# Three filler matmuls tied ahead of Q, and a new order of the work, in a gated mix of memory attention and a ReGLU layer

## The chip, the cores and the metric

The kernel runs on one NeuronCore of one Trainium2 chip. The metric is the device time of one execution in microseconds, as a median over runs. The engines are TensorE (PE, with its weight loads as PEld), VectorE (DVE), ScalarE (ACT), GpSimd (POOL) and SyncE (SP, which here only issues DMAs). Each takes its own instructions in order and waits on semaphores for the others.

## The reference

One sequence of 2048 tokens with 512 features goes through two branches, and a gate per token mixes them.

```python
g = sigmoid((x * gate_w).sum(-1))              # one number per token
# branch A: 32 heads of 16, in 4 segments of 512 tokens, M and z carried along
a_dot = softmax(q k^T * scale + mask) v        # causal, within the segment
a_mem = (phi(q) M) / (phi(q) z + 1e-6)         # recall of the segments before
o = sigmoid(beta) * a_mem + (1 - sigmoid(beta)) * a_dot
M += phi(k)^T v;  z += phi(k).sum(tokens)      # after each segment
a = o @ wo                                     # phi(t) = t + 1 if t > 0 else exp(t)
# branch B
b = (relu(x W_gate) * (x W_up)) @ W_down       # 512 -> 1792 -> 512
out = g * a + (1 - g) * b
```

All inputs and the output are bf16; sums are made in fp32 in PSUM.

## The kernel before

The four segments are processed one after another. For a segment the kernel has these pieces, each a task for one engine:

- Q and K projections for four groups of eight heads (`proj_q`, `proj_k`): four matmuls of 128x512 each (L460, in `full`), copied out of PSUM by DVE (L556 to QT, L572 to ktr, L575 to the masked KT). phi of them is an exponential on ACT and two operations on DVE (L529, L530). phi of K is transposed by a DMA on SP's queue (L588, pkT to pK).
- V projections for four blocks of 128 tokens (`proj_v`, copied by L602).
- Scores: 16 small matmuls per group (L623, and L636 for half blocks on the diagonal), 32 rows of the array each and four side by side. ACT does the exponential of 128x2048 (L645, to E). PSUM banks 0 to 3 are theirs, so one group of scores follows the exponential of the one before.
- Products with V (L696, 17 columns of the array each, four side by side), normalised on DVE (L727, L735, L737, L732, L708).
- Memory: the update (L816, L832), the denominators (L752), which go to DRAM and come back spread over partitions (L770 stores `coefs`, L784 reloads it to `cdr` and `xn`), the recall (L792) and its multiply on DVE (L803).
- The gate per token from `xn`, the rows of x (L414), which is loaded again for each segment (L276).
- The ReGLU layer: 14 pieces of gate and up matmuls, ReLU on ACT (L860, to `rgr`), the product on DVE (L866, to `hT`, 14 buffers), and for each 128 tokens 14 matmuls on `wd_sb` and 4 on `wo_sb` into one bank, scaled by L892 and stored by SP (L897).

A full-width matmul that stands behind column-tiled work is emitted by `full` as four matmuls of 32 columns (L464) side by side instead of one of 128 (L460), so that the tiling of the array does not change there.

What runs when is set by a list written into the kernel. The tasks are numbered as they are added to `Plan`; `ORDER` is the list of these numbers, and `UNITS` has one character for every use of a buffer and says which one of its ring or which PSUM bank is taken. A planner, which is not in the file, has made both from the tasks' estimated durations and from `lat`, the time until a result is seen elsewhere. `Plan.run` follows the list and asserts that a task stands behind those that it depends on. The order across engines comes from semaphores alone.

At the start, x of the first segment and `wq` are loaded by SP and ACT in eight transfers; then SP issues wk, wv and the other weights. PE does seven matmuls on constants (`heat`, L911). `x0_tasks` (L489 on) then transposes x on PE: 16 matmuls with an identity in five tasks (`flip`, L497), each with a copy out of PSUM on DVE or ACT (L505). With the last one it adds a task `idle` with fillers, matmuls on a zeroed tile `junk` (L515) whose result nobody reads. Q of the first segment waits for these copies and for `wq`.

Of the kernel before, what the change touches and what calls it, by code (L numbers as in the profile page):

```python
# [12 lines left out]
P = 128  # L13
# [14 lines left out]
RH = 14  # L28

ORDER = """  # L30
# [62 lines left out]
"""  # L93

UNITS = (
    "765432100132020000013101220024300002310000001000000012000000000300010000320000101003220101"
    "1333037221411293125003a1206013d023c0128200b00110010001000003000101111202000012221300456102"
    "1000000300000002300000000200000000021000212021042231103832220016112b200332370109023d102522"
    "6c010a100010003030007050103121103020013433212012450011000003200000002300000000210002000001"
    "00022313012212031271013301542062134310a1029420b0218202c113d1100001030206070303030202331200"  # L100
    "004563201000003200000003200000000010000000760000134203022222121201602230025023a504c3137312"
    "83119407b625d00110112100"
)


class Slot:


    def __init__(self, cands):
        self.cands, self.units, self.left = tuple(cands), (), 0  # L110

    @property
# [66 lines left out]
def kernel(  # L179
# [15 lines left out]
    nc = tc.nc  # L195
# [7 lines left out]
    plan = Plan()  # L203
# [285 lines left out]
    def x0_tasks():  # L489
        got = []  # L490
        parts = [(0, 0, 4), (1, 0, 4), (2, 0, 4), (3, 0, 2), (3, 2, 4)]
        for n, (t, c0, c1) in enumerate(parts):
# [17 lines left out]
            if n == 4:  # L510
                js = work()

                def idle(js=js):
                    for h in range(2):
                        nc.tensor.matmul(bank(js)[:, 2 * P * h:2 * P * h + 2 * P],  # L515
                                         lhsT=junk[:, 0:P],
                                         rhs=junk[:, None, 0:P].to_broadcast([P, 2, P]), start=True,
                                         stop=True)
                plan.add("PE", 426, K(-9) + n + 0.5, idle, [a], lat=0, need=[js], frees=[js], size=4)
            got.append(b)  # L520
        x0_first.extend(got[0:2])
        return [got[0:4], got[0:3] + got[4:5]]

    def proj_mm(w, c, seg):
# [452 lines left out]
```

## Time and profile before

| | |
|---|---|
| median of three runs | 267.53 us (267.46 to 268.33) |
| the profiled execution's own time | 268.72 us |
| its span, first to last instruction | 266.8 us |
| PE busy | 258.2 us (97%) |
| DVE busy | 204.2 us (77%) |
| ACT busy | 182.3 us (68%) |
| POOL busy | 63.7 us (24%) |
| moved by DMA | 19.43 MB, mean 73 GB/s |

A view by stage gives the busy time of each engine in a stretch, with the count of its instructions. A timeline gives start and length of a run of like instructions; the bracket behind it is the idle time before, and what ended it. In a list of groups, a row has the line of the kernel, the engine, the operation, the tiles and shapes, the count, then the busy time, the mean duration of one in ns, and the idle time in front of them. Matmuls are pipelined, so that the duration of one is longer than the step from one to the next. Some 30 of the matmuls have no record in this trace.

### The profile page before, as it was taken

How to read it: one execution, taken by the hardware profiler on the slowest of the kernel's cores; microseconds unless marked ns; L12 is line 12 of the kernel's file. 1: busy time of each engine (PE TensorE's matmuls, PEld its weight loads, DVE VectorE, ACT ScalarE, POOL GpSimd, SP SyncE). 2: the span in 40 equal slices, each digit the busy share in tenths (PEclk: the TensorE clock that was granted, in tenths of full speed). 3: DMA queues.
4: the chain of work that ended last, by engine and by line, in shares of the span. 5: the costliest groups of instructions: out<-in, count | busy, mean ns of one | idle time of the engine just before them, and what ended most of it. 6: DMA issues, size and time to landing. Idle time of an engine off the chain costs nothing.

```text
span 266.8 us, 8499 instructions
## 1 busy us (share of the span) xinstructions
PE 258.2 (97%) x3647; PEld 120.2 (45%) x3677; DVE 204.2 (77%) x473; ACT 182.3 (68%) x168; POOL 63.7 (24%) x168
## 2 busy tenths in 40 slices
PE   7999999999999999999999999999999999999995
PEld 4534444454445444444444444454444444445454
DVE  3499999999969476759999895768978875759422
ACT  3089998998886789883867777767466867761200
POOL 8023734132213222231122221222012222220000
PEclk9999999999999999999999999999999999999999
DMA  6999980111413410001101213200200120300011
GB/s 189 328 260 336 237 192 2 23 25 33 92 30 74 144 45 22 2 2 37 46 19 29 47 42 105 78 22 2 78 2 5 58 86 22 104 6 5 2 39 39
DMA packets 30028, 19.43 MB, mean 73 GB/s; under 512 B 15016, under 2 KB 28456, under 8 KB 29992
## 3 DMA queue, kind: packets, MB, share of 16 engines
q1 hardware_dynamic: 29416, 18.38, 24.8%
q8 instruction: 28, 0.46, 0.7%
q10 hardware_dynamic: 576, 0.52, 0.7%
q14 instruction: 8, 0.07, 0.1%
HBM read 13.21 MB, written 2.55 MB: 59 GB/s over the span
## 4 chain that ended last, share of the span: by engine, by line
PE 86%; DVE 8%; issue 3%; DMA 2%; SPq 0%; ACT 0%; DVEq 0%; ACTq 0%
PE ps L460 53%; PE ps L464 16%; PE ps L623 7%; PE ps L696 7%; DVE junk L414 2%; DMA wq_sb<-in_A_wq_dram 2%; DVE ktr L572 1%; DVE hT L866 1%; DVE KT L575 1%; PE ps L636 1%; PE ps L816 1%; DVE gcat L391 1%; DVE Vp L602 0%; PE ps L792 0%; PE ps L752 0%
## 5 line engine op out<-in xcount | busy, mean ns | idle before, releaser
L645 ACT ACTIVATE E<-ps 128x2048 bf16<-128x2048 f32 x64 | 120.3, 1880 | 28.0 <-PE ps L623 24.8
L674 POOL TENSOR_SCALAR_AFFINE_SELECT E<-E 128x256 bf16<-128x256 bf16 x128 | 53.9, 445 | 171.0 <-ACT E L645 171.0
L460 PE MATMUL ps<-xT,wg_sb 128*128 128x512 bf16 x179 | 50.3, 380 | 0.6 <-issue 0.3
L866 DVE TENSOR_TENSOR hT<-ps,rgr 128x512 bf16<-128x512 f32 x56 | 37.7, 683 | 15.8 <-PE ps L460 9.5
L460 PE MATMUL ps<-xT,wu_sb 128*128 128x512 bf16 x165 | 45.9, 380 | 0.4 <-issue 0.2
L860 ACT ACTIVATE rgr<-ps 128x512 bf16<-128x512 f32 x56 | 32.8, 599 | 17.6 <-PE ps L464 9.8
L460 PE MATMUL ps<-wd_sb,hT 128*128 128x512 bf16 (+2 forms) x168 | 37.5, 344 | 0.5 <-issue 0.5
L727 DVE STREAM_TRANSPOSE T<-ps 128x512 f32<-128x512 f32 x32 | 22.0, 707 | 7.3 <-PE ps L696 7.0
L460 PEld LDWEIGHTS <-wg_sb 128*128 128x128 bf16 x186 | 17.1, 98 | 21.7 <-issue 3.0
L623 PE MATMUL ps<-QT,KT 32*128 32x320 bf16 (+3 forms) x512 | 25.4, 273 | 0.3
L460 PEld LDWEIGHTS <-wu_sb 128*128 128x128 bf16 x170 | 15.4, 98 | 19.4 <-issue 2.8
L892 DVE TENSOR_SCALAR osr<-ps,ngcol 128x512 bf16<-128x512 f32 (+2 forms) x18 | 12.4, 688 | 14.0 <-PE ps L460 10.5
L460 PEld LDWEIGHTS <-hT 128*128 128x128 bf16 x174 | 15.4, 98 | 16.0 <-issue 1.5
L464 PE MATMUL ps<-wd_sb,hT 128*32 128x512 bf16 x312 | 20.5, 379 | 0.0
L696 PE MATMUL ps<-E,Vp 128*17 128x320 bf16 (+3 forms) x512 | 19.2, 273 | 0.4 <-DVE ktr L572 0.3
L623 PEld LDWEIGHTS <-KT 32*128 32x128 bf16 x512 | 7.7, 92 | 25.9 <-issue 25.0
L460 PE MATMUL ps<-xT,wq_sb 128*128 128x512 bf16 (+1 forms) x64 | 17.0, 394 | 0.9 <-DMA wq_sb<-in_A_wq_dram 0.7
L645 ACT ACTIVATE Em<-ps 128x2048 bf16<-128x2048 f32 x8 | 15.0, 1881 | 4.1 <-PE ps L636 4.0
L460 PE MATMUL ps<-xT,wk_sb 128*128 128x512 bf16 x58 | 16.9, 379 | 0.3 <-issue 0.2
L460 PE MATMUL ps<-wv_sb,xT 128*128 128x512 bf16 x54 | 15.8, 380 | 0.6 <-issue 0.6
L572 DVE CAST ktr<-ps 128x512 bf16<-128x512 f32 x16 | 11.0, 686 | 4.4 <-PE ps L460 4.4
L464 PE MATMUL ps<-xT,wu_sb 128*32 128x512 bf16 x216 | 14.3, 379 | 0.0
(102 smaller groups left out, 298.2 us busy)
## 6 DMA issues: line engine op xcount, KB each, us to landing
out_dram<-osr SPq DMA_DIRECT2D x15, 128.0 KB
wd_sb<-in_B_W_down_dram SPq DMA_DIRECT2D x2, 896.0 KB
xn<-in_A_x_dram SPq DMA_DIRECT2D x3, 512.0 KB
xn<-coefs SPq DMA_DIRECT2D x6, 256.0 KB
cdr<-coefs SPq DMA_DIRECT2D x6, 256.0 KB
wg_sb<-in_B_W_gate_dram SPq DMA_DIRECT2D x2, 512.0 KB
wu_sb<-in_B_W_up_dram SPq DMA_DIRECT2D x2, 512.0 KB
wg_sb<-in_B_W_gate_dram SPq DMA_DIRECT2D x2, 384.0 KB
```

What stands on the lines that cost most here:

```text
L414: zs.append(plan.add("DVE", 690, key, lambda t=t: nc.vector.scalar_tensor_tensor(junk[:], xn[:, t, :], 1.0, gwb[:], ALU.mult, ALU.mult, ac ...
L460: nc.tensor.matmul(out, lhsT=lhsT, rhs=rhs, start=start, stop=stop)
L464: nc.tensor.matmul(out[r], lhsT=lhsT[:, r], rhs=rhs, start=start, stop=stop, tile_position=(0, 32 * j))
L572: d = plan.add("DVE", 600, key - RQK, lambda: nc.vector.tensor_copy(ktr[ks.i][:], bank(sl)), [a], DVL + 40, need=[ks], frees=[sl])
L623: nc.tensor.matmul(ps[:, j * L + o:j * L + o + L - q], lhsT=KT[i][rows, kb, 3 * r:3 * r + 2].rearrange("p h q -> p (h q)"), rhs=QT[i][rows ...
L645: last_exp[0] = [plan.add("ACT", 66 + 4 * L / 1.2, key, lambda: nc.scalar.activation(dst, ps[:, 0:4 * L], ACT.Exp, scale=SCALE), [a] + war ...
L674: nc.gpsimd.affine_select(out=m[:, :, o:o + HP], in_=m[:, :, o:o + HP], compare_op=ALU.is_ge, fill=0.0, base=HP, pattern=[[0, 4], [1, HP]] ...
L696: nc.tensor.matmul(bank(sl)[32 * m:32 * m + HW, q:q + w], lhsT=(Vp[i] if n < 4 else Vm)[:, kb, r, 4 * c + j, 0:HW], rhs=rhs, start=(n == 0 ...
L727: done.append(plan.add("DVE", 633, key - RL, lambda r=r, sl=sl: nc.vector.transpose(T[ts.i][:, r], bank(sl)), [a] + done, 75 if r else 0, ...
L860: r = plan.add("ACT", 478, key - RL, lambda sl=gsl, rs=rs: nc.scalar.activation(rgr[rs.i][:], bank(sl), ACT.Relu), [g], ACL, frees=[gsl])
L866: nc.vector.tensor_tensor(hT[hs1.i][:], bank(sl), rgr[rs.i][:], ALU.mult)),
L892: nc.vector.tensor_scalar(osr[os.i][:, n0 - c0:n1 - c0], bank(sl)[:, 0:n1 - n0], ngcol[:, tt:tt + 1], None, ALU.mult)),
```

## The change

The fillers: there are three matmuls of 256 columns instead of two, all into the same half of a bank; the planner's duration for them is 640 ns instead of 426. The task's handle `j` is added to `x0_first`, the list of tasks for which the first matmuls of Q wait in the plan, so that the fillers have to stand ahead of Q.

The order: `ORDER` and `UNITS` are made anew. The planner took later times for the results of other engines, and of the free buffers of a ring it took the one that had been free for longest. The matmuls, copies and transfers that are done stay the same apart from the fillers, but PE's instructions change in number, since other matmuls now stand behind column-tiled work (3677 matmuls become 3969).

```diff
 ORDER = """
-    0 1 2 3 4 5 6 7 8 9 10 11 12 13 14 15 16 17 18 19 20 21 22 26 670 23 27 29 28 33 31 30 34
-    35 32 63 36 76 89 50 90 51 52 91 53 77 78 92 54 79 55 67 56 37 68 59 60 58 102 57 69 116 64
...
+    0 1 2 3 4 5 6 7 8 9 10 11 12 13 14 15 16 17 18 19 20 21 22 26 670 23 27 29 28 33 35 30 31
+    34 37 36 32 76 89 50 51 77 52 78 53 90 91 79 54 55 92 63 80 56 105 81 59 60 57 108 58 82
...
 UNITS = (
-    "765432100132020000013101220024300002310000001000000012000000000300010000320000101003220101"
...
+    "456701230142303000031221111122121222030000003000000010011000002300020000230113110223100023"
...
                 def idle(js=js):
-                    for h in range(2):
-                        nc.tensor.matmul(bank(js)[:, 2 * P * h:2 * P * h + 2 * P],
-                                         lhsT=junk[:, 0:P],
+                    for h in range(3):
+                        nc.tensor.matmul(bank(js)[:, 0:2 * P], lhsT=junk[:, 0:P],
                                          rhs=junk[:, None, 0:P].to_broadcast([P, 2, P]), start=True,
                                          stop=True)
-                plan.add("PE", 426, K(-9) + n + 0.5, idle, [a], lat=0, need=[js], frees=[js], size=4)
+                j = plan.add("PE", 640, K(-9) + n + 0.5, idle, [a], lat=0, need=[js], frees=[js],
+                             size=6)
             got.append(b)
-        x0_first.extend(got[0:2])
+        x0_first.extend(got[0:2] + [(j, 0.0)])
         return [got[0:4], got[0:3] + got[4:5]]
```

More of the change, by code (lines that the diff above doesn't have):

```diff
@@ L30 @@
 ORDER = """
[62 rows of a table removed]
[62 rows of a table added]
 """
 UNITS = (
-    "765432100132020000013101220024300002310000001000000012000000000300010000320000101003220101"
[L97 to L102, printed above, removed]
+    "456701230142303000031221111122121222030000003000000010011000002300020000230113110223100023"
+    "135121300042016323701290018020d320a211b001c00111002222003003111322000222203122100214567302"
+    "1000003300000003201100000200003000001011303031023221103821070016002332053209102a3224113b02"
+    "1d213c011211002010120122032121202030212232003145670132000002200000003301100000010000000033"
+    "01101302038322101272209312232232036211a0115110b3024103d022c1002120132212242202021113315302"
+    "135671032000002300000002301100000320000000120110238012130303027200901220233212600053214300"
+    "a302d024b211c01101200110"
 )
```

120 rows, old and new, of the table ORDER are left out of this document.

## The prediction

> **What bounds the kernel now.** I read the page first, for the engines' shares.
>
> ```profile
> span 266.8 us, 8499 instructions
> PE 258.2 (97%) x3647; PEld 120.2 (45%) x3677; DVE 204.2 (77%) x473; ACT 182.3 (68%) x168; POOL 63.7 (24%) x168
> ```
>
> TensorE (PE) is busy for 97% of the span. A change can gain only where PE idles, where it runs slowly, or in the tail. The busy time by stage says where that is:
>
> ```profile
> core 0: us, PE busy (x) PEld busy (x) DVE busy (x) ACT busy (x) POOL busy (x), PEclk, DMA share, GB/s
> 0.00:10.00 10.00, 8.45 (x38) 4.85 (x39) 2.37 (x11) 2.24 (x3) 5.46 (x24) 1.00 0.76 225
> 10.00:20.00 10.00, 9.67 (x65) 4.28 (x66) 9.24 (x23) 6.45 (x8) 1.82 (x4) 1.00 1.12 294
> 30.00:60.00 30.00, 29.57 (x512) 13.61 (x509) 28.82 (x74) 28.16 (x30) 11.37 (x33) 1.00 0.34 69
> 120.00:150.00 30.00, 29.29 (x297) 12.78 (x299) 28.22 (x70) 21.06 (x23) 6.63 (x12) 1.00 0.15 40
> ```
>
> The first 10 us lack 1.55 us of PE. After that PE lacks 0.33 us in ten, then 0.4 to 0.7 in each 30. From 30 to 60 us DVE (28.8 of 30) and ACT (28.2 of 30) are nearly full too, and DVE is again from 120 to 150. So the head is worth a look, and then PE's order in time there:
>
> ```profile
> 0.84 2.93 PE L911 MATMUL ps<-const-bfloat16-1.0 128*128 128x512 bf16 x7 [0.84 <-PEq L961]
> 3.57 1.91 PE L497 MATMUL ps<-ident,xn 128*128 128x128 bf16 x16
> 6.19 4.92 PE L460 MATMUL ps<-xT,wq_sb 128*128 128x256 bf16 x20 [0.71 <-DMA wq_sb<-in_A_wq_dram]
> 10.96 1.46 PE L460 MATMUL ps<-xT,wk_sb 128*128 128x512 bf16 x6
> 12.25 0.38 PE L515 MATMUL ps<-junk 128*128 128x256 bf16 x2
> 12.69 0.38 PE L460 MATMUL ps<-xT,wk_sb 128*128 128x512 bf16 x1
> 12.90 0.59 PE L460 MATMUL ps<-wv_sb,xT 128*128 128x512 bf16 x2
> 13.62 0.40 PE L623 MATMUL ps<-QT,KT 32*128 32x448 bf16 x8
> ```
>
> PE warms itself, transposes x, idles 0.71 us until wq has landed, and does Q. The two fillers (junk) stand at 12.25 us, not in that gap. Now the same shape early and late, first between 6 and 10 us, then between 10.4 and 13 us (the last figure before the second bar is the mean duration of one):
>
> ```profile
> L460 PE MATMUL ps<-xT,wq_sb 128*128 128x256 bf16 x12 | 2.7, 419 | 0.7 <-DMA wq_sb<-in_A_wq_dram 0.7
> L460 PE MATMUL ps<-xT,wq_sb 128*128 128x512 bf16 x3 | 1.5, 634 | 0.0
> L460 PE MATMUL ps<-xT,wk_sb 128*128 128x512 bf16 x7 | 1.8, 379 | 0.1
> L460 PE MATMUL ps<-xT,wq_sb 128*128 128x256 bf16 x2 | 0.4, 273 | 0.0
> ```
>
> Until about 10 us PE runs at about half rate, although the table's PEclk says 1.00. Six matmuls on wk take 1.46 us and one alone 0.38, so each further one costs (1.46 - 0.38) / 5 = 0.216 us. From 6.19 to 10.96 us PE does 14 matmuls of 256 columns and 6 of 512, 13 times 512 columns: 13 x 0.216 = 2.81 us at the full rate. It took 4.77. **The half rate costs Q 1.96 us.** Twice that, 3.9 us, is how long it lasts: until 6.19 + 3.92 = 10.1 us.
>
> **The change, part by part.**
>
> *The fillers move.* Two, of 2 x 0.109 = 0.22 us, leave the path at 12.25 us. Three stand between the last transpose and Q. At half rate each costs about 0.216 us, 0.65 in all; the transposes end at 5.48 us and Q starts at 6.19, so 0.07 us of the gap is left and wq still sets Q's start. If wq came up to 0.6 us sooner, the cover would be gone and Q would be held for that long. The fillers also wait for DVE: their bank is that of the first x tile, which DVE copies out from 4.24 us on, three copies in 1.76 us, so it is free by 4.9, before they are due:
>
> ```profile
> 4.24 1.76 DVE L505 CAST xT<-ps 128x512 bf16<-128x512 f32 x3 [2.64 <-PE ps L497]
> 9.90 1.95 DVE L556 CAST QT<-ps 128x512 bf16<-128x512 f32 x3 [3.90 <-PE ps L460]
> 12.02 0.69 DVE L572 CAST ktr<-ps 128x512 bf16<-128x512 f32 x1 [0.17 <-PE ps L460]
> ```
>
> *The full rate comes earlier.* 4.6 us of PE work without a break (0.84 to 5.48) did not bring it; 3.9 us after the break (6.19 to 10.1) did. [...] Q then runs at half rate for 0 to 0.8 us, which costs 0 to 0.4 instead of 1.96: a gain of 1.55 to 1.95, I take 1.7, a little under the middle. [...]
>
> *What is late next.* wv. The order has V's first matmul after 14 of 256 and 12 of 512 columns of Q and K, 19 x 0.216 = 4.1 us: it is wanted at 10.3 to 10.7, where before it was at 12.90. Its landing is not shown. x, wq, wk and wv are 2.1 MB, and by the GB/s of these rows (123 for 3 us, 262 for 3 us, then us by us) they are in by 9.6, or by 11 if other traffic shares the queues:
>
> ```profile
> 0.00:3.00 3.00, 2.16 (x6) 0.81 (x7) 0.51 (x7) 0.32 (x1) 2.16 (x10) 1.00 0.38 123
> 3.00:6.00 3.00, 2.48 (x19) 1.79 (x17) 1.76 (x3) 1.92 (x3) 2.80 (x12) 1.00 0.96 262
> ...
> 9.00:10.00 1.00, 1.00 (x3) 0.30 (x2) 0.10 (x1) 0.00 (x0) 0.00 (x0) 1.00 1.02 352
> 10.00:11.00 1.00, 1.00 (x7) 0.59 (x6) 1.00 (x2) 0.00 (x0) 0.00 (x0) 1.00 1.08 383
> ```
>
> The wait is 0 to 0.7; I take 0.3. Queued behind it on PE are the rest of K and V and the first scores (L623). These wait for K's chain on DVE: K's last matmul, the 0.69 us copy, three KT scalings; from K's copy at 12.02 to scores at 13.62 it was 1.6 us. Now K ends after 12 of 256 and 10 of 512 columns, about 10.1 with 0.2 lost to the half rate, its copy starts at about 10.3, and the scores could start at 11.9, which PE reaches at 12.0 without and 12.3 with the wait. The 0.19 us by which PE waited there before (12.90 + 2 x 0.216 + 0.1 for the switch of tiling, against 13.62) goes. Head: -0.22 - 1.7 + 0.3 - 0.19 = **-1.8 us**.
>
> *The new order.* In the built programs PE's matmuls are the same in columns, and both change the tiling 152 times. Between the first nine score groups the old order has 77 matmuls of 512 columns in the eight gaps, 10 in most; the new one has 95, mostly 12 or 14. After the last score group 122 become 106. So work is spread forward.
>
> ```profile
> L645 ACT ACTIVATE E<-ps 128x2048 bf16<-128x2048 f32 x64 | 120.3, 1880 | 28.0 <-PE ps L623 24.8
> L860 ACT ACTIVATE rgr<-ps 128x512 bf16<-128x512 f32 x56 | 32.8, 599 | 17.6 <-PE ps L464 9.8
> 140.88 0.73 PE ps L696 x32
> ```
>
> A gap of 10 is 2.2 us of PE plus scores of about 0.4; ACT needs 1.88 for the exponential and mostly a 0.60 for something else, 2.5 in all. There was no slack, and now there is 0.4 to 0.8 per gap. The work moved forward also raises DVE's and ACT's load early, so it is not free. On SP's queue one key transpose (pK) now goes ahead of the reload of xn:
>
> ```profile
> 33.15 0.49 SPq L276 DMA_DIRECT2D xn<-in_A_x_dram  x1
> 39.39 0.67 DVE L414 SCALAR_TENSOR_TENSOR junk<-xn,gwb 128x512 bf16<-128x512 bf16 x1
> ```
>
> Until about 31 us weights fill the DMA queues, so SP does not run ahead with PE. xn comes some 1.2 us later, and its user on DVE, L414, is due about as much earlier: DVE may stop for up to 1 us there, in a stage where it is full. That is in the bounds below. From 10 to 264 us PE lacks 264 - 10 - (258.2 - 8.45) = 4.2 us of busy time, some of it records that are missing; 140.88, where DVE's chain hands back to PE, is the largest stop. All 4.2 is the most that can be won. A loss is not excluded; I bound it by one such DVE stage again, 2 us. I take **-0.4**, nearer to zero, because few of these stops exceed 0.3 us.
>
> 97 more full-width matmuls are done as four of 32 columns. I take 0 by these rows:
>
> ```profile
> 241.72 15.32 PE ps L464 x284
> L464 PEld LDWEIGHTS <-hT 128*32 128x32 bf16 x312 | 7.8, 97 | 6.5 <-issue 0.3 <-DVE hT L866 0.2
> 263.97 0.35 DVE osr L892
> ```
>
> 284 / 4 = 71 quartets in 15.32 us are 0.216 each, the same as one whole matmul. The end is alike: two 128-column copies and one small output transfer behind the last matmul, 266.8 - 264.0 = 2.8 us.
>
> **Sum.** -1.8 - 0.4 = -2.2 us. The profiled execution's own time is 268.72 us (span 266.8 and 1.9 around it), 1.2 over the median of the three runs, 267.53. It would become 266.5, and the median 265.3.
>
> **Rivals.**
>
> *The break still counts.* [...] Then only the fillers' 0.22 and the order's 0.4 are gained: 266.9. [...] Against: 0.07 left of 0.71. Chance 0.16.
>
> *Slower: the last coefficients.* The new order does the third segment's memory update some 44 us of PE work later, so that the fourth's denominators, their round trip by DRAM and the recall stand close. On SP's queue the last reload (L784) now also stands behind an output transfer.
>
> ```profile
> 226.49 0.57 SPq L770 DMA_DIRECT2D coefs<-dnr  x1
> 228.97 1.20 SPq L784 DMA_DIRECT2D xn<-coefs  x2
> 163.59 1.20 SPq L784 DMA_DIRECT2D cdr<-coefs  x2
> 168.00:169.00 1.00, 1.00 (x40) 0.48 (x29) 1.00 (x3) 0.79 (x1) 0.14 (x1) 1.00 0.59 203
> 238.85 0.37 PE ps L792 x16
> ```
>
> Before, 12.4 us lay between store and recall; now 9.4 of PE work do. From the last reload to its user on DVE (L803) there are 7.4, and a reload takes at most 4.4 or so to issue and land (those issued at 163.59 keep the queues busy to about 169, with what lay ahead of them). If it slips past L803, DVE, in order, holds the last hT products and PE's last matmuls. Spare are about 2 to 3 us; to end over 0.8 us slower the slip must pass some 3 + 2.2 + 0.8 = 6 us, giving 268.5 or more. Chance 0.08.
>
> *Slower: quartets cost.* [...] In this trace four loads of 32 columns take 4 x 7.8 / 312 = 0.10 us of the load path. Were they uncovered, 97 x 0.10 = 9.7 us would be lost; the gain is used up from 0.023 each. 0.216 against 0.216 speaks against it. Chance 0.04.
>
> **How the numbers follow.** The forecast has 0.70, 0.02 stays unnamed. Its own range is head -1.2 to -2.4 and order +0.8 to -1.2, ends that hardly fall together: 264.2 to 267.0. With the first rival's spread I give 264.1 to 267.4. About 0.3%, 0.8 us, can be told from no change. Faster: 0.70 x 0.95 + 0.16 x 0.4 = 0.73. Same: 0.13, mostly the first rival. Slower: 0.14, the rest.
>
> **What would show it.** Right: fillers right behind the transposes, a gap below 0.1 us before Q, 256-column matmuls of Q near 273 ns from about 7 us on, first scores near 12.3 us, and PE's lack after 10 us below 4.2. Wrong: matmuls of 634 ns still at 9 us (first rival); a wait of over 0.7 us for wv; DVE's L803 waiting for a DMA near 235 us; quartets over 0.216 us.

## The result, and the profile after

The changed kernel takes **265.0 us** (median of six runs, 264.45 to 265.43), the kernel before 267.69 us (six runs, 267.28 to 268.69). The ratio is 0.9894, with a 95% interval of 0.9872 to 0.9917. The profiled execution took 264.89 us, with a span of 263.2. The forecast was 265.3. The sum came out, and the experiments show that two of its terms did not: most of the gain is not where the forecast put it.

The page of the changed kernel, with the lines on the shares and the chain that ended last:

```profile
span 263.2 us, 9091 instructions
PE 255.8 (97%) x3941; PEld 118.8 (45%) x3969; DVE 204.4 (78%) x473; ACT 183.2 (70%) x168; POOL 61.9 (24%) x168
PE 90%; DVE 4%; DMA 3%; issue 1%; SPq 0%; DVEq 0%
```

PE is the bound as before. The timeline of PE in the head, and the groups of matmuls between 6 and 10 us (last figure before the second bar: mean ns of one):

```profile
3.57 1.71 PE L497 MATMUL ps<-ident,xn 128*128 128x128 bf16 x16
5.12 0.49 PE L515 MATMUL ps<-junk 128*128 128x256 bf16 x3
5.69 2.87 PE L460 MATMUL ps<-xT,wq_sb 128*128 128x256 bf16 x18
9.49 0.38 PE L460 MATMUL ps<-xT,wk_sb 128*128 128x512 bf16 x1
10.42 0.60 PE L460 MATMUL ps<-wv_sb,xT 128*128 128x512 bf16 x2 [0.55 <-DMA wv_sb<-in_A_wv_dram]
11.82 0.40 PE L623 MATMUL ps<-QT,KT 32*128 32x448 bf16 x8
```

```profile
L460 PE MATMUL ps<-xT,wq_sb 128*128 128x256 bf16 x13 | 1.9, 273 | 0.0
L460 PE MATMUL ps<-xT,wq_sb 128*128 128x512 bf16 x6 | 1.6, 379 | 0.0
```

At first sight it is what was forecast: the fillers stand behind the transposes, Q runs at 273 ns where it had run at 419, V waits for wv, and the first scores come at 11.8 us instead of 13.6. (The second matmul on wk has no record ahead of that wait, while other profiles of this order show two there; the wait is therefore nearer to 0.33 us than to the 0.55 of the row.) But the fillers took 0.49 us together, 0.109 from one to the next: they ran at the full rate already. From the last transposes on, the step from one to the next is 56 ns instead of 107; the full rate came at 4.9 us, ahead of the fillers. So this profile does not show that they brought it.

Behind the head, the busy time by stage:

```profile
core 0: us, PE busy (x) PEld busy (x) DVE busy (x) ACT busy (x) POOL busy (x), PEclk, DMA share, GB/s
0.00:10.00 10.00, 8.94 (x51) 4.97 (x52) 4.67 (x14) 2.14 (x3) 5.46 (x24) 1.00 0.76 235
30.00:60.00 30.00, 29.58 (x534) 13.70 (x540) 28.20 (x69) 26.51 (x26) 9.46 (x28) 1.00 0.38 73
120.00:150.00 30.00, 29.58 (x369) 12.84 (x362) 26.15 (x63) 20.98 (x22) 5.47 (x14) 1.00 0.22 56
```

DVE has more room where it was nearly full: 28.20 us instead of 28.82 from 30 to 60, 26.15 instead of 28.22 from 120 to 150, and ACT 26.51 instead of 28.16. The matmuls done as quartets cost nothing here either. This is a run of 44, and the group behind it:

```profile
247.01 2.55 PE L464 MATMUL ps<-wd_sb,hT 128*32 128x512 bf16 x44
249.38 1.03 PE L464 MATMUL ps<-wo_sb,oT 128*32 128x512 bf16 x16
```

Eleven quartets take 249.38 - 247.01 = 2.37 us, 0.215 each.

### The profile page after: what moved, and what is told of

Same layout as the page of the kernel before. It is cut to its first block, busy times and chain, and to the rows that moved or that the text cites. A ratio compares the mean times of both kernels' runs of the same rounds, so it can differ in the third digit from the quotient of the medians.

```text
span 263.2 us, 9091 instructions
## 1 busy us (share of the span) xinstructions
PE 255.8 (97%) x3941; PEld 118.8 (45%) x3969; DVE 204.4 (78%) x473; ACT 183.2 (70%) x168; POOL 61.9 (24%) x168
## 4 chain that ended last, share of the span: by engine, by line
PE 90%; DVE 4%; DMA 3%; issue 1%; SPq 0%; DVEq 0%
PE ps L460 48%; PE ps L464 24%; PE ps L623 8%; PE ps L696 7%; DMA wv_sb<-in_A_wv_dram 2%; DMA xn<-in_A_x_dram 1%; PE ps L636 1%; PE ps L816 1%; DVE KT L575 1%; DVE ktr L572 1%; DVE junk L414 1%; PE ps L752 1%; DVE hT L866 0%; DVE gcat L391 0%; PE ps L792 0%
## 5 line engine op out<-in xcount | busy, mean ns | idle before, releaser
L645 ACT ACTIVATE E<-ps 128x2048 bf16<-128x2048 f32 x64 | 120.1, 1876 | 31.3 <-PE ps L623 27.1
L674 POOL TENSOR_SCALAR_AFFINE_SELECT E<-E 128x256 bf16<-128x256 bf16 x128 | 52.6, 435 | 171.5 <-ACT E L645 171.4
L460 PE MATMUL ps<-xT,wg_sb 128*128 128x512 bf16 x144 | 40.6, 380 | 1.0 <-issue 0.5
L460 PE MATMUL ps<-wd_sb,hT 128*128 128x512 bf16 (+1 forms) x161 | 37.8, 352 | 0.5 <-issue 0.5
L460 PE MATMUL ps<-xT,wu_sb 128*128 128x512 bf16 x133 | 36.4, 380 | 0.6 <-issue 0.5
L727 DVE STREAM_TRANSPOSE T<-ps 128x512 f32<-128x512 f32 x32 | 22.8, 712 | 12.0 <-PE ps L696 11.8
L464 PE MATMUL ps<-xT,wu_sb 128*32 128x512 bf16 x336 | 23.5, 379 | 0.0
L460 PEld LDWEIGHTS <-wg_sb 128*128 128x128 bf16 x152 | 13.9, 98 | 17.7 <-issue 2.4
L460 PEld LDWEIGHTS <-hT 128*128 128x128 bf16 x167 | 14.2, 98 | 16.0 <-issue 2.7
L460 PEld LDWEIGHTS <-wu_sb 128*128 128x128 bf16 x140 | 12.9, 98 | 16.1 <-issue 1.9
L464 PE MATMUL ps<-wd_sb,hT 128*32 128x512 bf16 (+1 forms) x340 | 20.0, 362 | 0.0
L464 PE MATMUL ps<-xT,wg_sb 128*32 128x512 bf16 x288 | 19.2, 379 | 0.0
L460 PE MATMUL ps<-xT,wq_sb 128*128 128x512 bf16 (+1 forms) x69 | 17.2, 355 | 0.3 <-issue 0.2
L645 ACT ACTIVATE Em<-ps 128x2048 bf16<-128x2048 f32 x8 | 15.1, 1882 | 3.3 <-PE ps L636 3.3
L460 PE MATMUL ps<-wv_sb,xT 128*128 128x512 bf16 x55 | 15.5, 379 | 0.6 <-DMA wv_sb<-in_A_wv_dram 0.6
L460 PE MATMUL ps<-xT,wk_sb 128*128 128x512 bf16 x50 | 14.3, 380 | 0.1
```

Source lines behind the costliest of these rows:

```text
L460: nc.tensor.matmul(out, lhsT=lhsT, rhs=rhs, start=start, stop=stop)
L464: nc.tensor.matmul(out[r], lhsT=lhsT[:, r], rhs=rhs, start=start, stop=stop, tile_position=(0, 32 * j))
L645: last_exp[0] = [plan.add("ACT", 66 + 4 * L / 1.2, key, lambda: nc.scalar.activation(dst, ps[:, 0:4 * L], ACT.Exp, scale=SCALE), [a] + war ...
L674: nc.gpsimd.affine_select(out=m[:, :, o:o + HP], in_=m[:, :, o:o + HP], compare_op=ALU.is_ge, fill=0.0, base=HP, pattern=[[0, 4], [1, HP]] ...
L727: done.append(plan.add("DVE", 633, key - RL, lambda r=r, sl=sl: nc.vector.transpose(T[ts.i][:, r], bank(sl)), [a] + done, 75 if r else 0, ...
```

## The experiments

Each kernel was timed in five rounds beside runs of the kernel before on the same chip. The medians of the kernel before differ between the four groups of runs (267.5 to 268.4 us), so the ratios are what is compared. The "lead" below is worked out from the traces: how much earlier than in the profile of before the same exponential of scores (L645) starts. Of long lines and lists the diffs show only what differs; three dots stand for what is left out.

| kernel | median us | ratio to before, 95% interval |
|---|---|---|
| changed kernel, first six runs | 265.0 | 0.9894 (0.9872 to 0.9917) |
| changed kernel, again | 265.33 | 0.9893 (0.9867 to 0.9919) |
| new order, no fillers | 265.64 | 0.9923 (0.9897 to 0.9949) |
| new order, fillers not tied | 265.66 | 0.9934 (0.9911 to 0.9957) |
| old order, three tied fillers | 268.18 | 1.0021 (0.9997 to 1.0045) |
| new order, no warming | 266.59 | 0.9931 (0.9905 to 0.9956) |
| old order, no warming | 268.51 | 1.0008 (0.9991 to 1.0025) |
| old order, buffer free for longest | 268.18 | 0.9989 (0.9968 to 1.0011) |
| new order, first free buffer | 277.22 | 1.0366 (1.0334 to 1.0397) |
| old order, xn first | 266.93 | 0.9958 (0.9935 to 0.9982) |
| old order, tied fillers, xn first | 267.37 | 0.9981 (0.9958 to 1.0005) |
| new order, V later | 265.01 | 0.9901 (0.9874 to 0.9928) |
| new order, nine fillers | 265.35 | 0.9902 (0.9872 to 0.9932) |

Theory A is the forecast: the fillers bridge the break, the full rate comes earlier by it, and that is most of the gain; without them the rate comes late again. Theory B: when the rate comes is chance. Theory C mixes the two. D (time won in the head of the old order is taken back behind it), E (the buffers made the gain) and F (the sequence made it) came up after the first group.

**One half of the change at a time.** First the new order without the fillers:

```diff
-                    for h in range(3):
+                    for h in range(0):
                         nc.tensor.matmul(bank(js)[:, 0:2 * P], lhsT=junk[:, 0:P],
```

> The new order with the filler loop empty. [...] Without them Q runs at half rate again to about 10 us, the head costs 1.5 us more, and the median is about 266.5; the matmuls of Q show 634 and 419 ns at 9 us. Theory B: where the grant falls against the kernel's start is chance, and bridging changes nothing. Then the median is within 0.3 us of the new kernel's 265.0, and the gain is the order's. [...]

Then the old order with the fillers, moved right behind the last transpose; in `UNITS` their bank becomes that of the new kernel:

```diff
-    35 32 63 36
+    35 37 32 63 36
...
-    56 37 68 59
+    56 68 59
...
-                    for h in range(2):
-                        nc.tensor.matmul(bank(js)[:, 2 * P * h:2 * P * h + 2 * P],
-                                         lhsT=junk[:, 0:P],
+                    for h in range(3):
+                        nc.tensor.matmul(bank(js)[:, 0:2 * P], lhsT=junk[:, 0:P],
```

> The old order with the three tied fillers alone (the idle task moved right behind the last transpose, bank as in the new kernel). Theory A: the head's 1.8 us are gained without the new order, about 265.9, and the order itself is worth the remaining 0.9. Theory B: only the two fillers leave the path at 12.25 us, 0.2 us, so 267.5 and within noise of the kernel before.

Measured: 0.9923 and 1.0021. The new order alone brings 0.0077 of 267.6 us, **2.1 us** (1.4 to 2.8). The fillers alone bring nothing, and may cost up to 1.2. That is not A, which wanted 1.8 us from the fillers. PE's head in the new order without fillers:

```profile
3.57 1.06 PE L497 MATMUL ps<-ident,xn 128*128 128x128 bf16 x8
5.20 1.04 PE L497 MATMUL ps<-ident,xn 128*128 128x128 bf16 x8 [0.57 <-DMA xn<-in_A_x_dram]
6.03 3.10 PE L460 MATMUL ps<-xT,wq_sb 128*128 128x256 bf16 x18
10.96 0.61 PE L460 MATMUL ps<-wv_sb,xT 128*128 128x512 bf16 x2 [0.32 <-DMA wv_sb<-in_A_wv_dram]
```

There is a break of 0.57 us in the transposes and no filler, and still 18 matmuls of Q take 3.10 us: the full rate came at about 6.2 us. The median lies 0.64 us above 265.0, where B allowed 0.3, so B did not come out whole. But none of the six runs lies near the 266.6 us that a late rate costs in this order (below), so its main point holds: the rate came early without the fillers. Where the rate came, by the step from one matmul to the next, in the 12 profiles of kernels that warm PE: at 3.8 to 6.3 us in 11 of them, with the break open (four) or filled or partly so (seven), and at 10.1 us in one, the profile of before from which the prediction was made.

**What a slow head costs.** To make the rate late on purpose, the seven matmuls on constants are left out, in both kernels:

```diff
     def heat():
         one = nc.const_aps.tensor(1.0, (P, 1), BF16)
-        for k in range(7):
+        for k in range(0):
```

The changed kernel was run again beside them, as the yardstick of this group:

> The changed kernel once more, unchanged, as the yardstick for the other kernels of this call. 264.9 to 265.1 by its first six runs. If the fillers are what brings the full rate early, Q runs at full rate from 7.7 us at the latest in this profile too.

And the two without warming:

> The new order and the fillers, but without the seven matmuls on constants at the start: PE begins with x's transposes at 3.57 us, so the full rate comes about 2.7 us later, and Q's first half runs at half rate, as in the profile of the old kernel. It prices a slow head in the new order. If head time counts in full there, Q's end moves by about 1.3 us, the 0.5 us of the wait for wv take up a part, and it is 0.8 to 1.5 us slower than the changed kernel: 265.8 to 266.5. If the loads of wk and wv set the head anyway: within 0.3 us.

> The old kernel without the seven matmuls on constants. It prices a slow head in the old order. Theory D: in the old order something behind the head (DVE and the exponentials from 30 to 60 us) sets the pace, and time lost or won in the head is taken up there; then it is within 0.4 us of the kernel before. The forecast's view that head time counts in full: 1 to 2 us slower, about 269.

Measured: the new order loses 266.59 - 265.33 = 1.26 us (1.0 by the ratios). The old order loses nothing (1.0008, 0.9991 to 1.0025). Here is Q's row from PE's timeline, of the new order and then of the old one:

```profile
6.00 3.60 PE L460 MATMUL ps<-xT,wq_sb 128*128 128x256 bf16 x18
```

```profile
6.59 4.50 PE L460 MATMUL ps<-xT,wq_sb 128*128 128x256 bf16 x20 [1.22 <-DMA wq_sb<-in_A_wq_dram]
```

Q is slow in both, in its first part in the new order and nearly throughout in the old one: from 6 to 10 us its matmuls of 256 columns take 360 and 417 ns in the mean, against 273 in the changed kernel. The old order without warming follows the profile of before to 0.03 us at every exponential, and 11 other profiles say that this head is the unusual one. Yet the median does not move. **In the old order time in the head is worth nothing; in the new one it is worth all of itself.** In the new order a delay that is there at the first exponential is there at the last: 0.54 us becomes 0.75 without fillers, 0.87 becomes 1.20 without warming.

**Buffers or sequence.** For each ring the choice is made when the list is run:

```diff
...
             for s in t.need:
+                if s.cands[0][0][0] != "ps":
+                    s.units = min((c for c in s.cands if not held & set(c)), key=lambda c: max(since.get(v, -1) for v in c))
                 assert not held & set(s.units)
...
                 if s.left == 0:
                     held -= set(s.units)
+                    since.update({v: len(done) for v in s.units})
```

> The old order, but for each ring the buffer that has been free for longest (PSUM banks as they were, fillers as they were). Theory E: the new kernel's gain behind the head comes from the choice of buffers; then 1 to 2 us of it show here, 265.6 to 266.6. Theory F: it comes from the sequence of the work; then within 0.4 us of the kernel before.

The other way round, the new order with `next(c for c in s.cands if not held & set(c))`:

> The new kernel with its order, but each ring's buffer is the first one free in the order instead of that which has been free for longest (PSUM banks as they are). If the spacing of the order carries the gain after 10 us, the time stays within 0.3 us of 265.0. If it comes from buffers that are reused later, writers wait for readers again and it is 0.5 to 1.5 us slower.

The old order gains nothing (0.9989, 0.9968 to 1.0011): theory F, the sequence. But the new order with the first free buffer loses 12 us, far more than either theory said. One DVE instruction, PE behind it, and PE's next matmuls (the lines stand two higher here: L531 is L529 of the changed kernel, L462 is L460):

```profile
36.91 0.29 DVE L531 TENSOR_SCALAR pkT<-ktr 128x512 bf16<-128x512 bf16 x1 [6.03 <-DMA pK<-pkT]
```

```profile
38.41 1.05 PE L466 MATMUL ps<-xT,wu_sb 128*32 128x512 bf16 x8 [4.76 <-DVE T L729]
40.76 1.91 PE L462 MATMUL ps<-xT,wk_sb 128*128 128x512 bf16 x4
```

DVE wants to write a `pkT` that a transposing DMA has yet to read, and stands for 6 us, since SP issues that DMA only at 33.89 us, behind the load of xT:

```profile
31.14 2.63 SPq L275 DMA_TRANSPOSE xT<-in_A_x_dram  x1
33.89 1.19 SPq L590 DMA_TRANSPOSE pK<-pkT  x1
```

PE idles 4.76 us and then pays again: four matmuls on wk take 1.91 us in the row above, where four took 1.04 in the changed kernel's head, and PE's clock reads 0.50 there (below). At the ninth exponential 7.6 of the 12 us are lost. So the longest-free choice gains nothing in the old order, and the new order needs it. Whether it would gain in the old order once the stop described next is gone was not run.

**Where the old order takes the lead back.** The profile of the old order with longest-free buffers has an early rate and a lead of 1.74 us, and ends at the span of before. Leads against the profile of before, at six of the 72 exponentials:

| exponential, and its start before | 1st, 14.07 | 11th, 41.02 | 12th, 43.87 | 15th, 51.94 | 27th, 87.32 | 72nd, 235.97 |
|---|---|---|---|---|---|---|
| old order, longest-free | 1.74 | 1.74 | 0.40 | 0.04 | -0.13 | 0.19 |
| old order, tied fillers | 2.08 | 2.07 | 1.50 | 1.45 | 0.16 | 0.14 |
| old order, tied, xn first | 1.95 | 1.95 | 1.95 | 1.95 | 1.17 | 1.18 |
| old order, xn first | 1.82 | 1.82 | 1.82 | 1.82 | 1.82 | 1.81 |

Between the 11th and the 12th stands this, in the first of them (its L417 is L414 of before, L575 is L572): DVE's timeline, and PE's waits with total us, times and the longest:

```profile
39.46 0.69 DVE L417 SCALAR_TENSOR_TENSOR junk<-xn,gwb 128x512 bf16<-128x512 bf16 x1 [1.73 <-DMA xn<-in_A_x_dram]
```

```profile
PE ps L467 <- DVE ktr L575: 1.2, 1, 1.2
```

DVE stops for 1.73 us until the reload of xn has landed. The copy of K to `ktr` stands behind, PE waits 1.2 us for it, and the lead is gone. That reload is tied to the weights and not to PE. Of SP's waits from 20 to 50 us, in the old order with tied fillers, this is the load of xT just ahead of it on SP's queue:

```profile
SPq L273 <- DMA wd_sb<-in_B_W_down_dram: 2.8, 1, 2.8
```

SP issues the load of xn at 34.70 us in the old order with longest-free buffers, at 33.71 with the tied fillers and at 33.15 in the profile of before, where DVE came to it at 39.39 us and did not wait. How much is lost may thus differ between executions. The 77 runs of the kernel before beside these experiments spread from 266.6 to 270.0 us, the 12 of the changed kernel from 264.5 to 266.2; that this is the reason is not shown. The stop predicts an experiment: exchange two loads on SP's queue, which one edit in the list does (339 is the load of xn, L276; 670 the transposing load of x, L273).

```diff
-    22 26 670 23 27
+    22 26 23 27
...
-    239 339 145
+    239 339 670 145
```

> The old kernel with the two loads on SP's queue exchanged and nothing else. By theory D its executions have an early head too, as long as the full rate came early, and lose it at xn: then 0.5 to 1.5 us faster than the kernel before. If the old kernel's executions have a late head as its profile has: within 0.3 us of it, since DVE came to xn there just when it had landed.

> The old order with the tied fillers, and on SP's queue the reload of xn (L276) ahead of the transposing load of x (L273) instead of behind it. Theory D: in the old order the 2 us won in the head are taken back because DVE stops for xn at 37 to 39 us (L414), and K's copy and V's stand behind that. Then the stop of 0.9 us for xn goes, the lead at the exponentials is still about 2 us after 45 us, where it had fallen to 1.2 to 1.5, and at least 0.8 us comes out at the end: 266.5 to 267.2. If the lead is lost all the same: at the old kernel's time, and something else than xn takes it.

Measured: 0.9958, so **1.1 us** (0.5 to 1.7) from nothing but that exchange, and with the tied fillers 0.9981 (unclear against before), against 1.0021 without the exchange. SP's rows in the second, then DVE's first L414 in the first:

```profile
32.62 0.39 SPq L276 DMA_DIRECT2D xn<-in_A_x_dram  x1
33.06 2.99 SPq L273 DMA_TRANSPOSE xT<-in_A_x_dram  x1
```

```profile
37.57 0.67 DVE L414 SCALAR_TENSOR_TENSOR junk<-xn,gwb 128x512 bf16<-128x512 bf16 x1
```

DVE is at xn 1.8 us sooner than in the profile of before and does not wait, and the lead of 1.82 us is whole at the end. That bears out theory D and shows where the lead is taken. With the tied fillers there is a second loss, 0.8 to 1.0 us between the 26th exponential and the 27th, in both kernels of the old order that have them. Here without and with xn first:

```profile
83.97 2.34 PE L464 MATMUL ps<-wd_sb,hT 128*32 128x512 bf16 x40 [0.84 <-issue]
```

```profile
82.95 2.34 PE L464 MATMUL ps<-wd_sb,hT 128*32 128x512 bf16 x40 [0.59 <-issue]
```

PE waits for nothing that the profile shows. Why it is longer with the fillers was not tried and stays open.

The new order is not immune to a late xn, it has room for one. DVE's waits from 20 to 60 us in the new order without fillers have

```profile
DVE junk L414 <- DMA xn<-in_A_x_dram: 0.9, 1, 0.9
```

and the exponentials lose 0.07 us by it, 0.54 becoming 0.61.

**The fillers themselves.** The same three fillers, moved from Q to just ahead of V's first matmul, and the tie in the plan taken out:

```diff
-    34 37 36 32
+    34 36 32
...
-    80 56 105 81
+    80 56 37 105 81
...
-        x0_first.extend(got[0:2] + [(j, 0.0)])
+        x0_first.extend(got[0:2])
```

> The new order with the same three fillers, but not tied ahead of Q: they stand right ahead of V's first matmul, where PE waits 0.5 us for wv in most profiles of this order, so that their own 0.33 us are covered there. The work is that of the new kernel; only the break before Q is open again. If filling the break is worth something, the median is 265.5 to 265.9, as without fillers (265.64). If the half rate is chance and the fillers only did no harm: 265.0 to 265.4, as the new kernel's two sets of runs (265.0 and 265.33).

And nine in place of three:

```diff
-                    for h in range(3):
+                    for h in range(9):
```

> The new kernel with nine fillers in place of three. The last transpose ends at about 5.3 us, nine take 1.0 us at the full rate and 1.9 at half, so that they end at 6.3 to 7.2, past the landing of wq at 5.7 to 6.2. If fillers cost nothing only while wq is late, Q starts 0.3 to 1 us later, of which the wait for wv takes up about 0.5: 0 to 0.5 us slower than the new kernel. If they hold PE's clock and were too few: faster.

Untied: 265.66 us. Taken with the kernel without fillers (12 runs) against the changed kernel (12 runs), the kernels without fillers in the gap are 0.46 us slower by the medians (0.12 to 0.83); by the ratios it is about 0.9, with intervals that overlap. The number is what "filling the break is worth something" wanted, but the break is not seen to be the reason: with the fillers untied Q is at the full rate all the same.

```profile
6.08 2.86 PE L460 MATMUL ps<-xT,wq_sb 128*128 128x256 bf16 x18 [0.59 <-DMA wq_sb<-in_A_wq_dram]
9.86 0.59 PE L460 MATMUL ps<-xT,wk_sb 128*128 128x512 bf16 x2
10.58 0.49 PE L515 MATMUL ps<-junk 128*128 128x256 bf16 x3
10.94 0.59 PE L460 MATMUL ps<-wv_sb,xT 128*128 128x512 bf16 x2
```

The second profile of the changed kernel has reached the same place at the same time, and goes on with V at once (one more matmul on wk has no record there; two take 2 x 0.216 = 0.43 us):

```profile
9.85 0.38 PE L460 MATMUL ps<-xT,wk_sb 128*128 128x512 bf16 x1
10.28 0.59 PE L460 MATMUL ps<-wv_sb,xT 128*128 128x512 bf16 x2
```

So the 0.66 us by which V starts later with the fillers untied (10.94 against 10.28) do not come from the break: the fillers themselves, 10.58 to 10.94, stand on the path instead of being covered, and 0.3 us pass ahead of them. Without fillers a part of x and wv landed later in the one profile there is. Nine fillers, ending at 6.08 us, cost nothing that can be told (0.9902 against 0.9893 and 0.9894). So 0.46 us lie between the kernels without and with fillers in the gap, and what an open break costs by itself stays open.

**Filling the wait for wv.** PE's order from 9 to 15 us is changed so that V's first four matmuls stand behind the rest of Q and of K:

```diff
-    63 80 56 105 81 59 60 57 108 58 82 116 64 61 65 117 109 84 67
+    63 80 56 81 59 60 57 64 58 82 65 105 116 61 117 108 109 84 67
```

> The new kernel with V's first four matmuls put behind Q's and K's remaining ones of the head, so that PE has work while wv lands. In the profile of the new kernel PE waits 0.55 us there for wv. If PE is the bound behind the head as well, the wait goes and 0.4 to 0.5 us with it: about 264.5. If K's copies on DVE or the exponentials set the pace from there on, the wait comes back ahead of the first scores or behind them, and the time stays within 0.2 us of 265.0.

0.9901 against 0.9893: no gain. The wait for wv is gone, and PE waits for wk instead:

```profile
9.92 0.61 PE L460 MATMUL ps<-xT,wk_sb 128*128 128x512 bf16 x2 [0.44 <-DMA wk_sb<-in_A_wk_dram]
```

Its first exponential starts 0.8 us later than in the changed kernel, 0.36 of it to the end. In this execution wq landed late too (Q at 6.20), so its profile alone does not price the edit; the ratio does. None of these kernels beats the changed one.

## Why the prediction was right, and where it was not

The time was right, 265.3 against 265.0, and so was the side, but two errors cancelled. By its steps:

**The full rate comes earlier, -1.7: failed.** The arithmetic on the profile of before was sound, but that execution was one in 12: in the other 11 the rate comes at 3.8 to 6.3 us, fillers or not. That filling the break brings the rate, and that Q is then at half rate for 0 to 0.8 us, was the author's estimate, and no run shows the term of -1.7. In its place the runs showed a rate that comes ahead of the fillers (at 4.9 us in the changed kernel), and a late one that costs the new order 1.26 us and the old one nothing. The rate comes up to 2.5 us apart in these 11, whose PE starts alike at 0.84 to 0.85 us; the prediction took one execution for all. That the break kept the rate away in the profile of before is neither shown nor excluded: breaks of 0.57 and 0.46 us shortly ahead of it did not keep it away in two profiles (new order without fillers, old order with xn first), and with the fillers untied it was there behind one of 0.59. Whether 0.71 kept it away, no run settles.

**Head time counts in full: failed for the order that it was worked out on.** The prediction took -1.8 as if it came out at the end of either order. In the old one it does not: tied fillers without the new order give no gain, and a slow head costs nothing (1.0008). The profile of before had no wait for xn to warn of this, since it showed the one head late enough to hide it. The prediction found the very place, L414 behind L276 on SP's queue, and had the sign turned: it feared a loss by that stop in the new order, and it is the old one that loses by it.

**The new order, -0.4: far too small.** Alone it measures -2.1 us (-1.4 to -2.8). The exchange of two loads, which only removes the stop for xn from the old order, gives 1.1 of the same kind. The rest was not tried one by one. PE's waits from 10 to 262 us in the old order with xn first, then in the changed kernel, show one piece of it, 140.88 us of the profile of before:

```profile
PE ps L696 <- DVE ktr L572: 0.3, 1, 0.3
PE ps L460 <- DVE hT L866: 0.2, 1, 0.2
```

```profile
PE ps L460 <- DMA wv_sb<-in_A_wv_dram: 0.6, 1, 0.6
PE ps L460 <- DVE hT L866: 0.2, 1, 0.2
```

The gaps between score groups, which the prediction counted (10 matmuls before, 12 to 14 after), are the likeliest reason for its room, but this is argued: that the new order lets a stop of 0.9 us on DVE pass is shown, and no run changes the gaps alone.

**What is late next: right in kind.** V waits about 0.33 us in the profile (0.3 taken, 0 to 0.7 given; the row's 0.55 includes a matmul without a record), and 0 in a second profile of the same kernel. Filling that wait does not pay, since PE then waits for wk.

**Fillers: off the path, right; never a cost, right** (nine cost nothing either). **Quartets, 0: right**, 0.215 us. **The end: right.** The rival of the last coefficients did not come: DVE was not idle ahead of L803.

**PE's lack.** Between 10 and 240 us PE lacked 230 - 225.86 = 4.1 us before and 3.4 after (the first row is of before):

```profile
10.00:240.00 230.00, 225.86 (x3212) 101.96 (x3240) 188.63 (x439) 177.21 (x160) 58.27 (x144) 1.00 0.26 72
```

```profile
10.00:240.00 230.00, 226.56 (x3466) 101.94 (x3497) 188.39 (x439) 179.30 (x162) 56.40 (x144) 1.00 0.27 72
```

By the forecast's own stretch, from 10 us to the last matmul, it is 4.2 before and 260.3 - 10 - (255.8 - 8.94) = 3.5 after. That is below 4.2 as forecast, and looks as if -0.4 were about right. It is not a test: of the two executions compared, only the one of before had the late head that keeps the old order's stops out of sight. The two errors, a head that was too dear and an order that was too cheap, are one error, and cancelled: what an early head loses in the old order was booked to the head. That the sum comes so close, -2.2 forecast and 265.0 - 267.69 = -2.7 measured, is luck.

## What to carry to other kernels

Before time saved early is counted, follow it to the first event whose time does not depend on the engine, here a reload behind the weights; if an engine in order stops there, the saving ends there, and the profile of a late execution does not show the stop. One profile is one draw of what differs between executions: a term that rests on when the full rate comes (here at 3.8 to 10.1 us in 12 profiles) needs a second execution, or a kernel that forces it late. Take the halves of a change apart even when the sum was right.

## What was not expected of the hardware

In one run PE's clock fell in the middle of the kernel, behind an idle time of PE, and there the profile says so: in the new order with the first free buffer, PE idles for 4.76 us, from 33.65 to 38.41, and the profile has this (PEclk is the third figure from the end):

```profile
37.00:38.00 1.00, 0.00 (x0) 0.00 (x0) 0.90 (x3) 0.00 (x0) 0.00 (x0) 0.53 0.79 226
42.00:43.00 1.00, 1.00 (x4) 0.40 (x3) 0.29 (x1) 0.51 (x1) 0.79 (x2) 0.50 0.00 0
43.00:44.00 1.00, 1.00 (x4) 0.34 (x3) 0.40 (x1) 0.56 (x1) 0.00 (x0) 0.56 0.00 0
44.00:45.00 1.00, 1.00 (x6) 0.30 (x6) 0.76 (x3) 0.07 (x1) 0.00 (x0) 1.00 0.00 0
```

Counted between 1.00 and 0.50, the means of 0.53 and 0.56 put the half rate's start at 37.06 and its end at 43.88 us: here it begins 3.4 us after PE fell idle and lasts 6.8 us, though PE works from 38.41 on. In the head of the profile of before the half rate reads 1.00 (419 ns for a matmul that takes 273 later), so there it has to be read off the steps between matmuls. What shorter idle times do to the clock was not tried.
